# Prologue of a spectral-mixing and MLP kernel: fewer fillers between the parts of x, matrices loaded beside x, two products moved from DVE to Pool, late groups reordered

## The chip, the cores and the metric

One core of one Trainium2 chip. The metric is the device time of one execution in microseconds (us). The profile's span runs from the first to the last instruction; the device time is 1.7 to 2.2 us more.

## The reference, cut to what matters

```python
X = np.fft.rfft(x, axis=1)                 # x: (8, 3008, 256) float32
Y = X * (filt_r + 1j * filt_i)[None]       # filters: (1505, 256)
a = np.fft.irfft(Y, n=3008, axis=1).reshape(24064, 256)
h = a @ w_in                               # 256 -> 2048
out = np.maximum(0.01 * h, h) @ w_out      # 2048 -> 256
```

## The kernel before

The transform of length 3008 = 94 x 32 is done in steps on TensorE: S1 (over 94), a 32x32 transpose T1 on DVE, S2 (over 32, with the f2 matrices), the filter product, SA (back), a transpose T2, SB (back over 94), which writes yt. For batch elements 1 to 7 all that is woven into the steady loop of the two large matmuls. For batch element 0 nothing can hide it: it is the prologue, and the loop's first matmul needs all of its yt. There, the 256 columns are done in two halves (hf 0 and 1), and each half has 24 values of k1 in groups.

```python
first_parts = ((0, 10), (10, 10), (20, 8), (28, 4))
for n0, nn in first_parts:
    x_load(0, n0, nn)                       # Pool queue, float32 to float16
for hf in range(2):
    filt_load(fa_sb, filt_r, hf * DH, DH)   # Pool queue
    filt_load(fb_sb, filt_i, hf * DH, DH)
    for i in (1, 0, 2) if hf == 0 else ():
        nc.gpsimd.dma_start(f2_sb[:, ts(i, NC // FP), :], f2_d.ap()[i])
nc.gpsimd.dma_start(w_in_sb[:], ...)
# ... cut ...
def first_s2(hf, c, n, kind, on_pool=False):    # n matmuls, then products with fa and fb
    ...
    if on_pool:                                 # ACT copies out of PSUM, Pool multiplies
        for j, xf in enumerate(xs):
            act(xf[:], ps[:, ts(j, 4), :])
        for i in range(2):
            for j, xf in enumerate(xs):
                nc.gpsimd.tensor_tensor(y[i][:, ts(j, 4), :], xf[:], fs[i][:, ts(j, 4), :], AL.mult)
    else:
        for i in range(2):
            nc.vector.tensor_tensor(y[i], ps, fs[i], AL.mult)

def first_sa(hf, c, n=4):                       # per 4 k1: two matmuls, one ACT cast
    ...
def upper(hf, t, copy):                         # upper 64 partitions of a filter
    copy(t[64:P, :, ts(hf, DH)], t[0:64, :, ts(hf, DH)])
def keep_warm(n):                               # n matmuls on zeros ("fillers")
    ...

keep_warm(14)
for n0, nn in first_parts:
    ...                                         # S1; copies on DVE and ACT by turns
    keep_warm(5 if n0 < N2 else 14)             # n0 is N2 after the last part
t1_part(0, 0, True)(), t1_part(0, 1, True)()
upper(0, fa_sb, act), upper(0, fb_sb, dve)
first_s2(0, 8, 8, "ph", True)
t1_part(0, 2, True)()
first_s2(0, 0, 8, "ph")
nc.sync.dma_start(i1_sb[:], i1_d.ap())
for n0 in (0, N2 // 2):
    x_load(1, n0, N2 // 2)
t1_part(0, 3, True)()
upper(1, fa_sb, act)
first_s2(0, 16, 4, "pf"), first_s2(0, 20, 4, "pf")
upper(1, fb_sb, dve)
keep_warm(4)
first_s2(1, 0, 8, "ph")
first_sa(0, 0, 8)
first_s2(1, 8, 8, "ph", True)
first_sa(0, 16), first_sa(0, 20), first_sa(0, 8, 8)
first_s2(1, 16, 4, "pf"), first_s2(1, 20, 4, "ph")
first_sa(1, 0, 8)
keep_warm(3)
first_t2(0), first_t2(1)
first_sa(1, 16), first_sa(1, 20), first_sa(1, 8, 8)
first_t2(2), first_t2(3)
# ... SB: 16 groups into yt, casts on ACT and DVE; then the loop ...
```

Of the kernel before, what the change touches and what calls it, by code (L numbers as in the profile page):

```python
# [18 lines left out]
N1, N2 = 94, 32  # L19
NC = 24  # L20
Q = 32
R1 = 96
FP = 3
# [46 lines left out]
def kernel(  # L70
# [9 lines left out]
    nc = tc.nc  # L80
# [12 lines left out]
    f2_d = nc.inline_tensor(f2_np, name="fwd2_const")  # L93
# [4 lines left out]
    f2_sb = cpool.tile([P, NC, P], FP16, name="f2_sb")  # L98
# [22 lines left out]
    def bank(kind, n, w):  # L121
        of = wide if kind == "ph" else single
        t = of[turn[kind] % len(of)]
        turn[kind] += 1
        return t[:, : n * w].rearrange("p (n w) -> p n w", n=n)
# [7 lines left out]
    def x_load(b, n0=0, nn=N2, d0=0, dn=D):  # L133

        for lo, cnt in ((0, R1),) if b + 1 < B else ((0, 64), (64, N1 - 64)):
            nc.gpsimd.dma_start(  # L136
                x_sb[lo : lo + cnt, ds(n0, nn), ds(d0, dn)],
                bass.AP(tensor=x.tensor, offset=x.offset + (b * N + lo * N2 + n0) * D + d0,
                        ap=[[N2 * D, cnt], [D, nn], [1, dn]]))

    def filt_load(dst, src, d0, dn):

        for q, first, sgn in ((0, 0, 1), (Q, N1, -1)):
            nc.gpsimd.dma_start(
                dst[q : q + Q, :, ds(d0, dn)],
                bass.AP(tensor=src.tensor, offset=src.offset + first * D + d0,
                        ap=[[N1 * D, N2 // 2], [sgn * NC * D, 2], [sgn * D, NC], [1, dn]]))


    nc.sync.dma_start(small_sb[:], small_d.ap())  # L150
    first_parts = ((0, 10), (10, 10), (20, 8), (28, 4))
    for n0, nn in first_parts:
        x_load(0, n0, nn)
    for hf in range(2):
        filt_load(fa_sb, filt_r, hf * DH, DH)
        filt_load(fb_sb, filt_i, hf * DH, DH)
        for i in (1, 0, 2) if hf == 0 else ():
            nc.gpsimd.dma_start(f2_sb[:, ts(i, NC // FP), :], f2_d.ap()[i])
    nc.gpsimd.dma_start(w_in_sb[:], moe_w_in.rearrange("(dt p) c -> p dt c", p=P))
    idle = cpool.tile([P, CH], FP16, name="idle")  # L160
    nc.vector.memset(idle[:], 0.0)
# [16 lines left out]
    def paired(t):  # L178
        return t[:].rearrange("p (e n t) -> p n e t", n=Q, t=2)
# [7 lines left out]
    def t1_part(b, i, flat=False):  # L187
        def go():
            a = big[(4 * b) % 3][:].bitcast(FP32)[:, ts(i, E4 * Q)].rearrange("p (e n) -> p e n", n=Q)
            o = big[(4 * b + 1) % 3][:].bitcast(FP32)  # L190
            if flat:
                o = o[:, ts(i, E4 * Q)].rearrange("p (e n) -> p e n", n=Q)
            else:
                o = o.rearrange("p (n e) -> p e n", n=Q)[:, ts(i, E4), :]
            nc.vector.transpose(o, a)  # L195
        return go
# [54 lines left out]
    def first_s1(n0, n, kind, copy):  # L251
        ps = bank(kind, n, D)
        for j in range(0, n, 2):
            nc.tensor.matmul(ps[:, ds(j, 2), :], fwd1[:N1], x_sb[:N1, ds(n0 + j, 2), :],  # L254
                             start=True, stop=True)
        spread(big[0], n0, ps, copy)
# [6 lines left out]
    def first_s2(hf, c, n, kind, on_pool=False):  # L263
        ps = bank(kind, n, DH)
        src = paired(big[1])
        for j in range(n):
            nc.tensor.matmul(ps[:, j, :].rearrange("p (e t) -> p e t", t=2), f2_sb[:, c + j, :],  # L267
                             src[:, c + j, ts(hf, DH // 2)], start=True, stop=True)
        fs = [f[:, ds(c, n), ts(hf, DH)] for f in (fa_sb, fb_sb)]
        y = [prods[hf][:, i, ds(c, n), :] for i in range(2)]  # L270
        if on_pool:
            xs = [scrp.tile([P, 4, DH], FP32, tag=f"p{j // 4 + 1}", name=f"fx_h{hf}_c{c + j}")
                  for j in range(0, n, 4)]
# [9 lines that stand above are left out]
    def first_sa(hf, c, n=4):  # L283
        y = [prods[hf][:, i, ds(c, n), :] for i in range(2)]
        for j in range(0, n, 4):
            ps = bank("pf", 4, DH)
            for i, m in enumerate((inv2, inv2x)):
                nc.tensor.matmul(ps, m, y[i][:, ds(j, 4), :], start=(i == 0), stop=(i == 1))  # L288
            act(paired(big[2])[:, ds(c + j, 4), ts(hf, DH // 2)],
                ps.rearrange("p n (t e) -> p n e t", t=2))  # L290
# [19 lines left out]
    def upper(hf, t, copy):  # L310
        copy(t[64:P, :, ts(hf, DH)], t[0:64, :, ts(hf, DH)])


    def keep_warm(n):
        for _ in range(n):
            nc.tensor.matmul(po_ps.rearrange("p a d -> p (a d)"), idle[:, 0:P], idle[:],  # L316
                             start=True, stop=True)

    keep_warm(14)
    g = 0  # L320
    for n0, nn in first_parts:
        while nn:
            n = 2 if nn % 4 or n0 >= N2 - 4 else 4
            first_s1(n0, n, two[n // 4], (dve, act)[g % 2])
            n0, nn, g = n0 + n, nn - n, g + 1
        keep_warm(5 if n0 < N2 else 14)
    t1_part(0, 0, True)(), t1_part(0, 1, True)()
    upper(0, fa_sb, act), upper(0, fb_sb, dve)
    first_s2(0, 8, 8, "ph", True)
# [2 lines left out]

    nc.vector.memset(i1_sb[:, 0, 0:2], 0.0)
    nc.sync.dma_start(i1_sb[:], i1_d.ap())
    for n0 in (0, N2 // 2):
        x_load(1, n0, N2 // 2)
    t1_part(0, 3, True)()
    upper(1, fa_sb, act)
    first_s2(0, 16, 4, "pf"), first_s2(0, 20, 4, "pf")
    upper(1, fb_sb, dve)  # L340
    keep_warm(4)
    first_s2(1, 0, 8, "ph")
    first_sa(0, 0, 8)
    first_s2(1, 8, 8, "ph", True)
    nc.gpsimd.dma_start(w_out_sb[:], moe_w_out.rearrange("(ct p) d -> p ct d", p=P))
    first_sa(0, 16), first_sa(0, 20), first_sa(0, 8, 8)
    first_s2(1, 16, 4, "pf"), first_s2(1, 20, 4, "ph")
    first_sa(1, 0, 8)
    keep_warm(3)
    first_t2(0), first_t2(1)  # L350
# [118 lines left out]
```

## Time and profile before

| | before |
|---|---|
| median of 3 runs | 780.63 us (780.33 to 781.06) |
| span | 778.8 us |
| first matmul on x | 7.07 |
| T1 starts (the "first transposes") | 14.77 |
| T2 starts (the "last transposes") | 31.57 |
| last copy into yt ends | 39.81 |

The page gives shares over the whole span. Only the engines' timelines, in order of time, tell about a stage of 39 us. A line of a timeline has the start, the duration, the engine, the source line, what it writes from what, how many, and in brackets the idle time before it with what ended it. Line numbers are those of the kernel shown; in the changed kernel the same line stands two or three further down. The profile leaves out the numbers in names: f2_sb stands there as f_sb, i1_sb as i_sb. This one, of TensorE in the kernel before, is worth a look before the prediction: L254 is S1, L316 the fillers.

```profile
7.07 0.38 PE L254 MATMUL pf<-x_sb,small_sb 94*128 94x512 f16 x1 [1.39 <-DMA x_sb<-in_x_dram]
10.38 1.24 PE L316 MATMUL po_ps<-idle 128*128 128x512 f16 x5
11.50 1.02 PE L254 MATMUL ph<-x_sb,small_sb 94*128 94x512 f16 x4
12.36 1.25 PE L316 MATMUL po_ps<-idle 128*128 128x512 f16 x5
13.44 0.60 PE L254 MATMUL pf<-x_sb,small_sb 94*128 94x512 f16 x2
```

The third and fourth parts of x are worked on right behind five fillers, with no wait for a DMA: there the fillers, not x, set the time.

### The profile page before, as it was taken

The numbers are of one execution on the slowest core, as the hardware profiler recorded it, in microseconds if no ns is written. First come the engines' busy times: TensorE is split into PE (matmuls) and PEld (weight loads), VectorE is DVE, ScalarE is ACT, GpSimd is POOL, SyncE is SP. The second block draws the span as 40 slices with busy tenths as digits, with TensorE's granted clock in tenths as the row PEclk, the third lists the DMA queues.
The fourth block names the chain that finished last, engine by engine and source line by source line (L and its number), as shares of the span: only waits on it lengthen the run. The fifth ranks groups of instructions, "written<-read, shape, count | busy, mean of one in ns | idle before, by whom it ended". The sixth has DMA issues, their size and how long they took to land.

```text
span 778.8 us, 13329 instructions
## 1 busy us (share of the span) xinstructions
PE 768.5 (99%) x5688; PEld 521.5 (67%) x5688; DVE 369.6 (47%) x468; ACT 553.5 (71%) x784; POOL 148.7 (19%) x123
## 2 busy tenths in 40 slices
PE   8899999999999999999999999999999999999998
PEld 4556666666776676666777667666667667666666
DVE  5989742765238641576407743187523764200000
ACT  5777768676787768777686775967668676666663
POOL 6854200330005200042002410025000330000000
PEclk9999999999999999999999999999999999999999
DMA  9951013210151010510105010230101010110111
GB/s 186 227 92 56 28 41 71 66 42 29 41 108 42 28 41 28 116 35 28 42 28 122 28 41 29 53 96 28 41 28 42 28 38 31 41 42 28 41 41 55
DMA packets 36154, 43.36 MB, mean 56 GB/s; under 512 B 8130, under 2 KB 34370, under 8 KB 35330
## 3 DMA queue, kind: packets, MB, share of 16 engines
q0 software_dynamic: 10208, 17.01, 12.4%
q1 hardware_dynamic: 25888, 25.52, 9.3%
q8 instruction: 44, 0.72, 0.4%
q14 instruction: 14, 0.11, 0.1%
HBM read 34.10 MB, written 24.64 MB: 75 GB/s over the span
## 4 chain that ended last, share of the span: by engine, by line
PE 96%; DVE 2%; ACT 1%; DMA 1%; issue 0%; DVEq 0%; POOLq 0%
PE ph L377 41%; PE po_ps L391 41%; PE pf L173 3%; PE pf L241 2%; PE pf L213 2%; PE pf L229 2%; PE pf L391 1%; DMA x_sb<-in_x_dram 1%; DVE big L195 1%; DVE prod L281 1%; PE pf L288 0%; ACT big L183 0%; PE po_ps L316 0%; PE ph L267 0%; PE ph L254 0%
## 5 line engine op out<-in xcount | busy, mean ns | idle before, releaser
L382 ACT ACTIVATE gt_c<-ph 128x1024 f16<-128x1024 f32 x376 | 384.9, 1024 | 195.5 <-PE ph L377 193.4
L377 PE MATMUL ph<-yt,w_in_sb 128*128 128x512 f16 (+3 forms) x1600 | 386.6, 367 | 0.3
L391 PE MATMUL po_ps<-w_out_sb,gt_c 128*128 128x256 f16 x2944 | 381.5, 273 | 0.5 <-ACT ost_c_t L398 0.5
L391 PEld LDWEIGHTS <-gt_c 128*128 128x128 f16 x3008 | 290.5, 98 | 82.3 <-issue 2.4
L377 PEld LDWEIGHTS <-w_in_sb 128*128 128x128 f16 x1600 | 154.4, 98 | 97.5 <-issue 0.4
L222 POOL TENSOR_TENSOR y_b_g<-p_b_g,p_b_g 128x512 f16<-128x512 f32 x84 | 106.8, 1272 | 225.7 <-DVE p_b_g L220 225.7
L195 DVE STREAM_TRANSPOSE big<-big 128x1024 f32<-128x1024 f32 x32 | 56.0, 1846 | 126.0 <-ACT big L183 125.9
L183 ACT CAST big<-pf 128x512 f16<-128x512 f32 x186 | 106.6, 605 | 1.1 <-PE pf L254 1.1
L244 DVE CAST yt<-pf 128x376 f16<-128x376 f32 x112 | 56.4, 545 | 86.0 <-PE pf L241 86.0
L218 DVE TENSOR_TENSOR p_b_g<-pf,fa_sb 128x512 f32<-128x512 f32 x84 | 58.1, 692 | 38.3 <-PE pf L213 35.3
L398 ACT COPY ost_c_t<-po_ps 128x256 f32<-128x256 f32 x184 | 69.4, 377 | 6.6 <-PE po_ps L391 5.4
L203 DVE STREAM_TRANSPOSE big<-big 128x1024 f32<-128x1024 f32 x28 | 51.1, 1936 | 34.0 <-ACT big L183 34.0
L219 DVE TENSOR_TENSOR p_b_g<-pf,fb_sb 64x512 f32<-64x512 f32 x84 | 58.2, 692 | 1.1
L220 DVE TENSOR_TENSOR p_b_g<-pf,fb_sb 64x512 f32<-64x512 f32 x84 | 57.4, 683 | 1.1
L136 POOL DMA_DIRECT2D x_sb<-in_x_dram x13 | 7.1, 548 | 253.7 <-PE pf L173 252.9
L241 PEld LDWEIGHTS <-big 128*128 128x128 f16 x448 | 25.7, 98 | 13.2
L173 PE MATMUL pf<-x_sb,small_sb 94*128 94x512 f16 x112 | 33.6, 380 | 0.2 <-DVE yt L244 0.2
L213 PE MATMUL pf<-big,f_sb 128*128 128x256 f16 x168 | 32.1, 273 | 0.0
L229 PE MATMUL pf<-y_b_g,small_sb 128*128 128x512 f16 x84 | 31.9, 380 | 0.0
L213 PEld LDWEIGHTS <-f_sb 128*128 128x128 f16 x168 | 16.4, 98 | 19.7
L241 PE MATMUL pf<-i_sb,big 128*128 128x94 f16 x448 | 28.7, 206 | 0.0
L173 PEld LDWEIGHTS <-small_sb 94*128 94x128 f16 x112 | 10.7, 98 | 10.5
(50 smaller groups left out, 166.8 us busy)
## 6 DMA issues: line engine op xcount, KB each, us to landing
out_dram<-ost_c_t SPq DMA_DIRECT2D x92, 256.0 KB, 2.1
x_sb<-in_x_dram POOLq DMA_DIRECT2D x5, 1536.0 KB, 11.1
x_sb<-in_x_dram POOLq DMA_DIRECT2D x2, 768.0 KB, 12.1
x_sb<-in_x_dram POOLq DMA_DIRECT2D x3, 480.0 KB, 7.3
w_in_sb<-in_moe_w_in_dram POOLq DMA_DIRECT2D x1, 1024.0 KB, 13.3
w_out_sb<-in_moe_w_out_dram POOLq DMA_DIRECT2D x1, 1024.0 KB, 11.8
x_sb<-in_x_dram POOLq DMA_DIRECT2D x1, 1024.0 KB, 8.1
fa_sb<-in_filt_r_dram POOLq DMA_DIRECT2D x4, 192.0 KB, 8.5
```

The costliest lines, as they stand in the source:

```text
L173: nc.tensor.matmul(ps, fwd1[:N1], x_sb[:N1, ds(2 * g, 2), :], start=True, stop=True)
L183: copy(paired(dst)[:, ds(n0, nn), ds(e0, de)], ps.rearrange("p n (e t) -> p n e t", t=2))
L195: nc.vector.transpose(o, a)
L213: nc.tensor.matmul(ps[:, j, :], f2_sb[:, 2 * g + j, :], src[:, 2 * g + j, :], start=True, stop=True)
L218: nc.vector.tensor_tensor(p1[:], ps, fa, AL.mult)
L219: nc.vector.tensor_tensor(p2[0:64], ps[64:P], fb[64:P], AL.mult)
L222: nc.gpsimd.tensor_tensor(y1[:], p1[:], p2[:], AL.add)
L241: nc.tensor.matmul(ps[:, j, :], src[:, dt, n2, :], i1_sb[:, n2, :], start=True, stop=True)
L377: nc.tensor.matmul(ph[:, j, ds(o, ln)], w_in_sb[:, dt, ts(ct, P)], yt[:, dt, ds(lo, ln)], start=(dt == 0), stop=(dt == NDT - 1),)
L382: nc.scalar.activation(gts[ci][:, ds(2 * g, 2), :], ph, AF.Lrelu)
L391: nc.tensor.matmul(po, gts[ci][:, ct, ts(tj, P)], w_out_sb[:, ct, :], start=(ct == 0), stop=(ct == NCT - 1))
L398: nc.scalar.copy(ost[:, tj % 2, :], po)
```

## The change

Its intent: spend fewer fillers where x has landed already; have the S2 matrices early by loading two parts of f2 on the SP queue beside x; relieve DVE of two filter products (k1 = 16 to 19 of the first half) by giving them to Pool; and put the last S2 group, in one wide piece, ahead of the SA groups, so that DVE doesn't wait for it.

```diff
--- before.py
+++ after.py
@@ -148,14 +148,16 @@
 
 
     nc.sync.dma_start(small_sb[:], small_d.ap())
+    for i in (1, 0):
+        nc.sync.dma_start(f2_sb[:, ts(i, NC // FP), :], f2_d.ap()[i])
     first_parts = ((0, 10), (10, 10), (20, 8), (28, 4))
     for n0, nn in first_parts:
         x_load(0, n0, nn)
     for hf in range(2):
         filt_load(fa_sb, filt_r, hf * DH, DH)
         filt_load(fb_sb, filt_i, hf * DH, DH)
-        for i in (1, 0, 2) if hf == 0 else ():
-            nc.gpsimd.dma_start(f2_sb[:, ts(i, NC // FP), :], f2_d.ap()[i])
+        if hf == 0:
+            nc.gpsimd.dma_start(f2_sb[:, ts(2, NC // FP), :], f2_d.ap()[2])
     nc.gpsimd.dma_start(w_in_sb[:], moe_w_in.rearrange("(dt p) c -> p dt c", p=P))
     idle = cpool.tile([P, CH], FP16, name="idle")
     nc.vector.memset(idle[:], 0.0)
@@ -316,14 +318,14 @@
             nc.tensor.matmul(po_ps.rearrange("p a d -> p (a d)"), idle[:, 0:P], idle[:],
                              start=True, stop=True)
 
-    keep_warm(14)
+    keep_warm(18)
     g = 0
-    for n0, nn in first_parts:
+    for (n0, nn), fill in zip(first_parts, (4, 3, 1, 14)):
         while nn:
             n = 2 if nn % 4 or n0 >= N2 - 4 else 4
             first_s1(n0, n, two[n // 4], (dve, act)[g % 2])
             n0, nn, g = n0 + n, nn - n, g + 1
-        keep_warm(5 if n0 < N2 else 14)
+        keep_warm(fill)
     t1_part(0, 0, True)(), t1_part(0, 1, True)()
     upper(0, fa_sb, act), upper(0, fb_sb, dve)
     first_s2(0, 8, 8, "ph", True)
@@ -332,19 +334,20 @@
 
     nc.vector.memset(i1_sb[:, 0, 0:2], 0.0)
     nc.sync.dma_start(i1_sb[:], i1_d.ap())
+    first_s2(0, 16, 4, "pf", True)
     for n0 in (0, N2 // 2):
         x_load(1, n0, N2 // 2)
     t1_part(0, 3, True)()
+    first_s2(0, 20, 4, "pf")
     upper(1, fa_sb, act)
-    first_s2(0, 16, 4, "pf"), first_s2(0, 20, 4, "pf")
     upper(1, fb_sb, dve)
     keep_warm(4)
+    first_s2(1, 8, 8, "ph", True)
     first_s2(1, 0, 8, "ph")
     first_sa(0, 0, 8)
-    first_s2(1, 8, 8, "ph", True)
+    first_s2(1, 16, 8, "ph")
     nc.gpsimd.dma_start(w_out_sb[:], moe_w_out.rearrange("(ct p) d -> p ct d", p=P))
-    first_sa(0, 16), first_sa(0, 20), first_sa(0, 8, 8)
-    first_s2(1, 16, 4, "pf"), first_s2(1, 20, 4, "ph")
+    first_sa(0, 20), first_sa(0, 8, 8), first_sa(0, 16)
     first_sa(1, 0, 8)
     keep_warm(3)
     first_t2(0), first_t2(1)
```

## The prediction

> **What bounds the kernel now.** I read the page first: engine shares, then the chain that ended last, then the costliest groups.
>
> ```profile
> span 778.8 us, 13329 instructions
> PE 768.5 (99%) x5688; PEld 521.5 (67%) x5688; DVE 369.6 (47%) x468; ACT 553.5 (71%) x784; POOL 148.7 (19%) x123
> PE 96%; DVE 2%; ACT 1%; DMA 1%; issue 0%; DVEq 0%; POOLq 0%
> ```
>
> TensorE is busy throughout and carries 96% of the chain. The change touches nothing in the steady loop, only what stands before its first matmul, so the next view is busy time by stretch (columns: stretch, length, busy PE, weight loads, DVE, ACT, Pool with counts, granted clock, DMA share, GB/s).
>
> ```profile
> 17.19:23.73 6.54, 4.53 (x37) 3.73 (x38) 6.51 (x8) 4.14 (x4) 5.87 (x6) 1.00 1.58 198
> 23.73:31.57 7.84, 7.84 (x40) 4.22 (x39) 7.17 (x11) 5.61 (x11) 5.70 (x7) 0.78 1.08 270
> 39.36:778.80 739.44, 734.88 (x5420) 502.47 (x5419) 340.59 (x433) 528.70 (x748) 119.36 (x92) 1.00 0.17 48
> ```
>
> From 39.36 on 739.44 us are TensorE's own, 734.88 of them busy. These don't change; what the change can win or lose is inside the first 39.4 us, and carries to the end one for one. In those stretches DVE is the full one (6.51 of 6.54, 7.17 of 7.84). The chain in order of time says the same for 14.8 to 24 us, then goes over TensorE, DVE and ACT. The timelines of the engines (start, duration, what, idle before and its releaser) fix the points that matter:
>
> ```profile
> 14.07 0.66 ACT L183 CAST big<-pf 128x512 f16<-128x512 f32 x1 [0.48 <-PE pf L254]
> 14.77 2.37 DVE L195 STREAM_TRANSPOSE big<-big 128x1024 f32<-128x1024 f32 x2 [0.21 <-ACT big L183]
> 14.52 0.71 POOL L144 DMA_DIRECT2D fb_sb<-in_filt_i_dram  x1 [0.35 <-DMA fa_sb<-in_filt_r_dram]
> 16.94 1.33 POOL L159 DMA_DIRECT2D w_in_sb<-in_moe_w_in_dram  x1 [0.56 <-DMA fb_sb<-in_filt_i_dram]
> 17.18 2.52 PEld L267 LDWEIGHTS <-f_sb 128*128 128x128 f16 x24 [0.62 <-DMA f_sb<-fwd_const]
> ...
> 29.16 0.69 DVE L281 TENSOR_TENSOR prod<-pf,fa_sb 128x512 f16<-128x512 f32 x1 [0.61 <-PE pf L267]
> 29.97 1.12 ACT L289 CAST big<-pf 128x512 f16<-128x512 f32 x2 [0.65 <-PE pf L288]
> 31.48 2.25 ACT L289 CAST big<-pf 128x512 f16<-128x512 f32 x4 [0.39 <-PE pf L288]
> 31.57 4.61 DVE L296 STREAM_TRANSPOSE big<-big 128x1024 f32<-128x1024 f32 x4
> 34.47 0.85 ACT L308 CAST yt<-pf 128x376 f16<-128x376 f32 x2 [0.73 <-PE pf L305]
> 39.26 0.55 DVE L308 CAST yt<-ph 128x376 f16<-128x376 f32 x1
> ```
>
> The first transposes wait for the last cast of x. Three landings then stand close together: the second half of fa_sb's first columns (Pool is released at 14.52), fb_sb's (16.94, so landed some 0.25 earlier), and the first part of f2 (17.18). DVE copies fb_sb's upper half at 17.17. The last transposes, four in a row, run from 31.57 to 36.18, and the last yt copy ends at 39.81.
>
> **What the Trainium skill says.** "TensorE: Matmul & The Clock Gate", Part 1: the clock is either full or half, judged over free-running windows of about 3.4 us. The trace agrees: 0.50 in all half-microsecond stretches from 24.5 to 27.5, after TensorE idled from 20.86 to 22.87. "DMA: Bandwidth & Descriptors", Queues, rings and completion order: an engine round-robins between the queues that have work, packet by packet. No run here shows it yet for the prologue; it is what the moved f2 loads will meet. "GPSIMD Engine Reference", 4.1 Engine selection: no PSUM access and about 2 times slower than VectorE with two inputs. Here it is 1.13 us against 0.67 for 128x512 (1.7 times), and an ACT copy of 0.53 stands ahead of it.
>
> **The change part by part.** I name the S2 groups by half and first k1, (half, k1).
>
> Zero-tile matmuls. The third part of x has landed when Pool is released at 11.39, the fourth at 12.38; the matmuls on them start at 11.50 and 13.44, behind five fillers of 0.216. With three and one fillers they could start at about 11.2 and 12.5. Then ACT and DVE copies queue (1.23 and 1.03 for wide, 0.66 for narrow), so the first transposes could start at about 13.95 instead of 14.77: 0.82 earlier. Four more fillers at the start end at 6.5, before x.
>
> f2 on the SP queue. Two loads of 256 KB leave before x instead of behind the filters. At the 0.8 us apiece which they take as they arrive in sequence, that is up to 1.3 to 1.6 us of all 16 DMA engines. Between 2 and 4 us only 92 to 101 GB/s move, against some 200 later, so part of it is hidden. I call what remains d and take d = 0.4 (0 to 1.0). All of x and the first filters land d later. The second filters then land about 1.6 - d earlier. That removes f2's wait at 17.18, but fb_sb's landing at 16.7 stays: DVE's upper copy starts at 16.7 + d = 17.1 against 17.17. So the 0.82 of the first step is nearly all lost at that next wait.
>
> k1 = 16 to 19 on Pool. DVE loses two products of 128x512, 1.24 us spacing. Pool gains two of 1.12, ACT one copy of 0.53 at a time when it waited 1.52 for a filter anyway. Pool: start about 18.1 + d, four products 4.45, two 2.24, x loads 1.1, four products 4.5: done at 30.4 + d = 30.8, against 31.16 now.
>
> The wide last group. Four products (29.16 to 31.65, 2.49) become two of 1.23 (2.40). As S2(1,16) now stands ahead of the late SA groups, DVE's 0.61 wait goes. DVE: 17.1, then 5.56 to the end of the fourth transpose (the spacing now, 17.17 to 22.73), 1.18, 0.99, 2.38, 2.40: last transposes could start at 29.6 against 31.57, a gain of 2.0 on DVE alone.
>
> But ACT has still the same twelve casts of SA, 0.58 each, to do after its copies for S2(1,8). The fourth transpose ends at 22.7, eight S2 matmuls take 1.0, ACT's copies 23.9 to 24.9. The first SA cast can start at about 25.4 (0.65 behind its matmul, as at 23.73 to 24.38 now). Then 12 x 0.58 = 7.0, and a hole of 0.7 while TensorE does S2(1,16): ACT ends at 33.1 to 33.3 with a full clock, against 33.73. If the clock is half again after the idle time (20.5 to 22.7 by the same spacing, 2.2 us, as long as now), the four SA matmuls ahead of S2(1,16) cost 1.7 instead of 0.9, and ACT ends at about 34.0. The third of the last transposes needs all of ACT's casts; it starts at 33.3 or 34.0 against 33.87 now.
>
> From there the yt copies: ACT's first eight begin when its SA casts end (33.4 or 34.0 against 34.47), and DVE's begin when the transposes end and a matmul has run, about 0.65 after: 36.25 or 36.95 against 36.92 now. Then 2.89 to the last copy, as now. Sum: 0.65 earlier with the full clock, nothing with the half clock. Even chances of both give 0.3. A mostly later cold window, or d nearer to zero, adds up to 0.5. I put the gain at 0.55, above the plain mean, because the order of SA groups (20, then 8, then 16) looks fitted to when Pool is done and I may have charged ACT's hole too fully. 780.63 - 0.55 = 780.1.
>
> **The rivals.** First, DVE is the bound and its saving arrives whole: 2.0 at the last transposes, 1.5 or so at the loop, 779.0. For it: DVE is the full engine of the prologue and waits just 0.61 in the middle. Against it: ACT's casts end only 0.14 before the third last transpose even now, and their number stays. Second, the f2 loads delay x by the whole 1.3: then everything from the first matmul is 0.9 later than I take, and the time is 780.6 to 781.3. For it: x's packets keep the DMA engines at a share near 1 from 4.5 us on. Against it: the thin stretch at 2 to 4 us. Third, Pool becomes the end of the chain: SA(1,8) waits for its products at 30.4 + d; with d = 1 and the x loads' issue longer, its two casts end at 33.3, so 0.5 of gain remains at most. Fourth, the steady loop shifts, by yt arriving in another order or x's second batch element landing late. Pool issues that at about 25 to 26 instead of 23.4, and it is used from 40.5; the DMA queue is full with w_in until about 30 in any case. I expect nothing of it.
>
> **Range and chances.** The gains of these lie between -0.5 and 1.6, and the three runs of before spread over 0.7 us. So 779.1 to 780.9 should hold it 8 times in 10. Two per cent is 15.6 us, 40% of the whole prologue: nothing here does that. Faster 0.01, same 0.985, slower 0.005.
>
> **What would show it.** The matmuls on x's first part at 7.1 + d; first transposes near 14.3; DVE's upper fb_sb copy waiting for a DMA, near 17.1; no wait of weight loads for f2. DVE's last transposes in two pairs with a gap between, the second pair released by ACT's SA cast, near 33.3 to 34. The loop's first matmuls at about 38.8, against 39.36, and 739.4 us after. I am wrong if the four transposes run without a gap from 30 on (the first rival), if x's first part starts after 7.9 (the second), if the third transpose is released by way of Pool's products, or if the stretch behind the loop's start differs from 739.4 by over 0.3.

## The result, and the profile after

| | before | changed |
|---|---|---|
| median, 4 runs each | 780.48 us (779.75 to 781.06) | 779.99 us (779.97 to 780.97) |
| ratio | | 0.9997, interval 0.998 to 1.0015: same |
| span | 778.8 | 777.8 |
| first matmul on x | 7.07 | 7.60 |
| first transposes | 14.77 | 15.09 |
| last transposes | 31.57, four in a row | 30.29, then 33.67 |
| last copy into yt ends | 39.81 | 39.20 |

A ratio is the mean time of one kernel's fast runs over that of the other's of the same rounds, so it isn't quite the ratio of the medians.

The timeline of TensorE in the changed kernel, at the same places (L256 is S1, L318 the fillers):

```profile
7.60 0.38 PE L256 MATMUL pf<-x_sb,small_sb 94*128 94x512 f16 x1
10.24 0.38 PE L256 MATMUL pf<-x_sb,small_sb 94*128 94x512 f16 x1 [0.53 <-DMA x_sb<-in_x_dram]
12.44 1.02 PE L256 MATMUL ph<-x_sb,small_sb 94*128 94x512 f16 x4 [0.31 <-DVE big L185]
13.52 0.59 PE L256 MATMUL pf<-x_sb,small_sb 94*128 94x512 f16 x2
```

The four parts start 0.53, 0.94, 0.94 and 0.08 later than before. Their landings in the trace say the same: 7.55, 10.19, 12.04 and 12.85, for 7.03, 9.26, 11.11 and 12.10. The fillers have become fewer, and x has become later: the second part is now waited for, and the third waits 0.31 for DVE to empty a bank that the late second part filled.

The timelines of DVE and ACT in the changed kernel, from the first transposes on:

```profile
15.09 2.37 DVE L197 STREAM_TRANSPOSE big<-big 128x1024 f32<-128x1024 f32 x2 [0.20 <-ACT big L185]
17.50 0.95 DVE L313 COPY fb_sb<-fb_sb 64x3072 f16<-64x3072 f16 x1
...
28.01 1.21 DVE L283 TENSOR_TENSOR prod<-ph,fa_sb 128x1024 f16<-128x1024 f32 x1
30.29 2.37 DVE L298 STREAM_TRANSPOSE big<-big 128x1024 f32<-128x1024 f32 x2
33.67 2.37 DVE L298 STREAM_TRANSPOSE big<-big 128x1024 f32<-128x1024 f32 x2 [1.01 <-ACT big L291]
...
28.15 3.14 ACT L291 CAST big<-pf 128x512 f16<-128x512 f32 x6 [0.71 <-PE pf L290]
31.51 2.13 ACT L291 CAST big<-pf 128x512 f16<-128x512 f32 x4 [0.21 <-PE pf L290]
33.62 0.85 ACT L310 CAST yt<-pf 128x376 f16<-128x376 f32 x2
38.65 0.55 DVE L310 CAST yt<-ph 128x376 f16<-128x376 f32 x1
```

DVE's wait for the late S2 group is gone and its last transposes start 1.28 earlier. But they no longer run in a row: the second pair waits 1.01 for ACT's SA casts, and starts about when the third of the four did before. Of 1.28 us won on DVE, 0.61 arrives at the last copy into yt. Two things more are seen in the lines of Pool and of the copies into yt (changed, then before, then changed):

```profile
24.86 1.86 POOL L280 TENSOR_TENSOR prod<-fx_h_c,fb_sb 128x512 f16<-128x512 f32 x1
30.03 2.27 POOL L280 TENSOR_TENSOR prod<-fx_h_c,fb_sb 128x512 f16<-128x512 f32 x2
...
36.92 1.01 DVE L308 CAST yt<-pf 128x376 f16<-128x376 f32 x2 [0.74 <-ACT yt L308]
38.17 0.55 DVE L308 CAST yt<-ph 128x376 f16<-128x376 f32 x1 [0.25 <-PE ph L305]
...
36.66 1.01 DVE L310 CAST yt<-pf 128x376 f16<-128x376 f32 x2 [0.61 <-PE pf L307]
37.58 0.54 DVE L310 CAST yt<-ph 128x376 f16<-128x376 f32 x1
```

Pool's last product ends at 32.30, 1.14 later than before. And of the 0.61, only 0.26 is there when DVE begins its copies into yt. The other 0.35 comes behind that: from there to the end it takes 2.54 in place of 2.89. ACT's first eight copies into yt begin and end 0.85 earlier than before (33.62 to 36.72, for 34.47 to 37.57), so that they are nearly done when DVE's begin, and DVE's wait of 0.25 is gone. All ten profiles with two separate pairs of last transposes have 2.54 or 2.55 here, the four without 2.80 to 2.90.

And the loop? The view of busy time by stretch in the changed kernel:

```profile
23.72:30.29 6.57, 6.57 (x38) 3.84 (x37) 6.51 (x6) 4.42 (x9) 6.56 (x8) 0.78 1.04 259
38.60:777.80 739.20, 734.89 (x5421) 502.41 (x5420) 340.52 (x433) 528.72 (x748) 121.29 (x92) 1.00 0.17 48
```

In the stretch ahead of the last transposes (23.72 to 30.29) Pool is busy for 6.56 of 6.57 us and DVE for 6.51; ACT, the releaser of the second pair, only for 4.42. TensorE's busy time in the loop is the same to 0.01 us. More exactly: from the end of the last copy into yt to the start of the last matmul it is 735.06 us in this profile, in that of before and, within 0.02, in all twelve experiments. So a profile's span is the end of that copy, plus 735.06, plus what follows the last matmul. The latter is 3.89 before and 3.56 in the changed kernel, an item that I come back to. With spans of 778.76 and 777.82 unrounded: 0.61 from the prologue and 0.33 from the program's end. Yet the device times of the two profiled runs, 780.54 and 779.99, differ by 0.55 only: what lies outside the span is 1.78 in the one and 2.17 in the other.

### The profile page after: what moved, and what is told of

Read it like the earlier page. It is cut to its first block, busy times and chain, and to the rows that moved or that the text cites. A ratio compares the mean times of both kernels' runs of the same rounds, so it can differ in the third digit from the quotient of the medians.

```text
span 777.8 us, 13325 instructions
## 1 busy us (share of the span) xinstructions
PE 768.4 (99%) x5685; PEld 521.3 (67%) x5685; DVE 368.4 (47%) x464; ACT 553.7 (71%) x785; POOL 149.9 (19%) x123
## 3 DMA queue, kind: packets, MB, share of 16 engines
HBM read 34.10 MB, written 24.64 MB: 76 GB/s over the span
## 4 chain that ended last, share of the span: by engine, by line
PE 95%; DVE 1%; ACT 1%; DMA 1%; issue 0%; POOL 0%; DVEq 0%; POOLq 0%
PE ph L380 41%; PE po_ps L394 41%; PE pf L175 3%; PE pf L243 2%; PE pf L215 2%; PE pf L231 2%; DMA x_sb<-in_x_dram 1%; PE pf L394 1%; PE pf L290 1%; PE ph L269 1%; ACT big L185 1%; DVE big L197 0%; DVE big L298 0%; DVE prod L283 0%; ACT big L291 0%
```

## The experiments

All were correct. Each was run five times beside the kernel before on the same chip; there were three batches, each on a chip of its own, and before with the half-clock window has means of 780.76, 780.68 and 780.77 on them. The landmarks of their profiles, in us (T0 is the start of the first transposes, "end" that of the last copy into yt, "rest" the time after the last matmul's start up to the span's end):

| profile | clock window | first matmul on x | T0 | last transposes | end | T0 to end | rest |
|---|---|---|---|---|---|---|---|
| before | half | 7.07 | 14.77 | 31.57, no gap | 39.81 | 25.04 | 3.89 |
| before_warm | full | 7.37 | 15.08 | 31.24, no gap | 39.49 | 24.41 | 3.90 |
| f2_alone | full | 7.74 | 15.68 | 31.83, no gap | 40.07 | 24.39 | 3.78 |
| changed | half | 7.60 | 15.09 | 30.29, 33.67 | 39.20 | 24.11 | 3.56 |
| again | half | 7.97 | 15.08 | 30.49, 33.90 | 39.42 | 24.34 | 3.56 |
| warm | full | 8.05 | 15.36 | 30.55, 33.68 | 39.22 | 23.86 | 3.56 |
| f2_old | full | 6.84 | 13.96 | 29.71, 32.84 | 38.37 | 24.41 | 3.68 |
| fill_old | half | 7.71 | 15.67 | 30.90, 34.31 | 39.85 | 24.18 | 3.56 |
| pool_old | half, twice as long | 7.67 | 14.99 | 32.02, 35.42 | 40.95 | 25.96 | 3.56 |
| pool_late | half | 7.79 | 15.15 | 31.74, 34.45 | 39.98 | 24.83 | 3.56 |
| order_old | half | 7.73 | 15.08 | 32.11, no gap | 40.35 | 25.27 | 3.55 |
| sa_dve | half | 7.95 | 15.22 | 30.71, 34.10 | 39.63 | 24.41 | 3.56 |
| best | full | 7.08 | 14.20 | 30.08, 32.79 | 38.33 | 24.13 | 3.68 |
| best_tail | full | 6.88 | 13.99 | 29.88, 32.59 | 38.12 | 24.13 | 3.33 |

"Half" means that the trace records 3.41 us of half clock in the prologue (6.83 in pool_old). Medians, and the ratio to the kernel before in the same rounds: again 780.21 (0.9998), f2_old 779.35 (0.9987), fill_old 780.59 (1.0001), pool_old 781.15 (1.0009), warm 779.85 (0.9992), before_warm 779.98 (0.9993), pool_late 780.47 (1.0003), best 779.01 (0.9981), f2_alone 780.83 (1.0009), order_old 780.67 (1.0003), sa_dve 780.02 (0.9996), best_tail 778.52 (0.9977). The intervals of f2_old, best and best_tail alone lie wholly below 1 (up to 0.9999, 0.9993, 0.9989). Smaller effects rest on the profiles' landmarks and on the groups of runs. Sorted by clock, the means are, with the half-clock window: before 780.73, changed 780.28, f2_old 779.55, fill_old 780.65, pool_late 780.71, order_old 780.87, sa_dve 780.12; at full clock: before 779.85, f2_old 779.29, best 779.00. Some of these groups have only two to four runs.

### again: the changed kernel, unedited

> The changed kernel once more, unedited, for the spread. The four runs so far are 779.97, 779.98, 779.99 and 780.97, those of the kernel before 779.75 to 781.06. If the phase of the clock's windows against the start of the kernel is what parts them (one theory), the times fall in two or three groups about 0.5 to 1 us apart in both kernels, and a profile in another group has its half-clock window elsewhere. If it is noise of the chip (the rival), they scatter evenly. Median expected at 780.0, ratio to before 0.9993, interval within 0.998 to 1.001.

Measured 780.11 to 780.77, all with a clock of 0.997 or 0.998. The kernel before gave two groups in this batch: 779.48, 779.55 and 779.70 at a clock of 1.000, and six from 780.53 to 781.06 at 0.997 to 0.998. Over all 27 runs of before with a known clock: ten at full clock with a mean of 779.85 and 17 with the half-clock window with a mean of 780.73. All nine of the changed kernel have the window; their mean is 780.28. So against before in the same clock, the changed kernel is 0.45 faster; against the mixture, 780.41, only 0.13. In the second profile of the changed kernel the window stands 0.90 later (24.13 against 23.23), and DVE's copy of fb_sb waits for its load, as predicted, which it had not done in the first:

```profile
15.08 2.37 DVE L197 STREAM_TRANSPOSE big<-big 128x1024 f32<-128x1024 f32 x2 [0.23 <-ACT big L185]
17.68 0.95 DVE L313 COPY fb_sb<-fb_sb 64x3072 f16<-64x3072 f16 x1 [0.23 <-DMA fb_sb<-in_filt_i_dram]
```

### f2_old: the f2 loads back on the Pool queue

```diff
-    for i in (1, 0):
-        nc.sync.dma_start(f2_sb[:, ts(i, NC // FP), :], f2_d.ap()[i])
-        if hf == 0:
-            nc.gpsimd.dma_start(f2_sb[:, ts(2, NC // FP), :], f2_d.ap()[2])
+        for i in (1, 0, 2) if hf == 0 else ():
+            nc.gpsimd.dma_start(f2_sb[:, ts(i, NC // FP), :], f2_d.ap()[i])
```

> The changed kernel, with the f2 loads put back behind the filters on the Pool queue; new fillers, Pool group and order stay. My theory: the f2 loads on the SP queue cost x its landings 0.5 to 0.95 us, so here the first transposes start at about 13.95 (15.09 in the changed kernel), weight loads of S2 wait for f2 until about 17.1, and DVE's upper copy starts at about 16.95 (17.50). Last yt copy ends about 0.4 to 0.5 earlier than the 39.20 of the changed kernel, so about 38.75 and 779.5. Rival: x's delay is the launch-to-launch state of the memory and not f2, then the first transposes stay at 15.1 or so and S2 starts when they end.

```profile
13.96 2.37 DVE L195 STREAM_TRANSPOSE big<-big 128x1024 f32<-128x1024 f32 x2 [0.22 <-ACT big L183]
16.53 0.95 DVE L311 COPY fb_sb<-fb_sb 64x3072 f16<-64x3072 f16 x1 [0.20 <-DMA fb_sb<-in_filt_i_dram]
16.96 1.92 PE L267 MATMUL ph<-big,f_sb 128*128 128x128 f16 x16 [0.97 <-DMA f_sb<-fwd_const]
32.84 2.37 DVE L296 STREAM_TRANSPOSE big<-big 128x1024 f32<-128x1024 f32 x2 [0.77 <-ACT big L289]
```

The lines of DVE and TensorE in this run confirm the direction, and the transposes to the tenth: they start at 13.96, and the wait for f2, 0.97 here, is back. The copy of fb_sb (16.53) and the end (38.37) come 0.4 earlier than I expected. Undoing this part makes the changed kernel 0.86 faster (median 779.35 against 780.21 of the same batch). Part of that could be the clock, which was full in the profile; but the three runs with a half-clock window have a mean of 779.55 against 780.32 of again, where all have it: still 0.77. The fillers' gain does exist, then: it shows when f2 isn't in x's way. It isn't the whole 0.82, though. The transposes start 0.81 earlier than in before, of which 0.23 is x itself, landing earlier in this profile; from the first matmul on x to the transposes it takes 7.70 in before and 7.12 here, in best and in best_tail 7.11. So the fillers give 0.58.

How the loads meet can be counted in the trace's records of DMA packets of the changed kernel (not a view of the profile, so a plain table; queue, packets, KB and median time of one, in the half microsecond from the time given; some left out):

```
from     x and filters (Pool queue)      constants (SP queue)
2.5      none                            46 packets,  92 KB,  84 ns
3.0      13 packets,  65 KB, 560 ns      69 packets, 112 KB,  84 ns
4.0      18 packets,  90 KB, 398 ns      16 packets,  32 KB,  96 ns
5.0      16 packets,  80 KB, 449 ns      14 packets,  28 KB,  96 ns
6.0      17 packets,  55 KB, 398 ns      22 packets,  44 KB,  96 ns
7.0      21 packets,  90 KB, 398 ns      19 packets,  24 KB,  84 ns
```

Once x's packets of 5120 bytes are there, f2's of 2048 bytes go beside them in about equal numbers, until nearly 8 us: about 16 of each in half a microsecond, which is what 16 engines give that take turns one by one (0.398 + 0.096 is 0.49 us for a pair). The trace doesn't tell the engine of a packet, so the turns are inferred from these counts. The first f2 load is issued at 1.14, ahead of x, and lands at 4.25. The second is issued at 1.61, behind x's first part (1.24), and lands at 8.63, also behind it (7.55): it takes 0.1 us of every half one, spread over all of x's first part and some of its second.

### fill_old: the old fillers

```diff
-    keep_warm(18)
+    keep_warm(14)
-    for (n0, nn), fill in zip(first_parts, (4, 3, 1, 14)):
+    for (n0, nn), fill in zip(first_parts, (5, 5, 5, 14)):
```

> The changed kernel with the old fillers (14, then 5 5 5). My theory: with x's parts landing as late as they do in the changed kernel, fillers 5 after the first and second part end as x lands and cost about 0 to 0.1, the third 5 delays the last two matmuls on x by four fillers, 0.86. First transposes at about 15.9 to 16.0 (15.09), last yt copy 0.7 to 0.9 later than 39.20, time 780.8. Rival: the DMA landings of the filters gate what follows anyway, then the end moves by under 0.3.

T0 is 15.67, 0.58 later than in the changed kernel and not 0.8 to 0.9, and the end 0.65 or 0.43 later than in the changed kernel's two profiles; the median is 0.38 above again's. The bound had shifted: in the changed kernel DVE's copies had already eaten part of what fewer fillers give. The rival, under 0.3, falls.

### pool_old and pool_late: k1 = 16 to 19 on DVE again

```diff
# pool_old
-    first_s2(0, 16, 4, "pf", True)
+    first_s2(0, 16, 4, "pf")
# pool_late
-    first_s2(0, 16, 4, "pf", True)
     ...
     t1_part(0, 3, True)()
-    first_s2(0, 20, 4, "pf")
+    first_s2(0, 16, 4, "pf"), first_s2(0, 20, 4, "pf")
```

> The changed kernel with k1 = 16 to 19 on DVE again, as before. Rival that DVE is the bound: its 1.24 us come back whole, the last yt copy ends at about 40.4 and the time is 781.2. My theory that ACT's twelve SA casts bind: ACT loses a copy of 0.53 that stood in a wait, Pool ends 2.2 earlier, DVE's last transposes run without a gap from about 31.5 to 36.1, which is where the second pair ends now (36.04): the last yt copy moves by 0 to 0.3, time 780.0 to 780.3. Third theory, that Pool binds the last SA groups (its products end at 32.25 in the changed kernel, and the last casts at 33.64): then the last casts come up to 1 us earlier.

This was a miss: the end came 1.75 later than in the changed kernel, more than the 1.24 of the products themselves. I had put the products ahead of the fourth transpose, where the changed kernel's code has the group; in the kernel before they stood behind it. Everything of the second half hangs on that transpose: it started at 23.18 in place of 21.90. And with the longer idle time of TensorE the half-clock window was twice as long. The run answers another question than I meant to ask. So the next puts them where they had been:

> The run pool_old put the products of k1 = 16 to 19 on DVE ahead of the fourth transpose, which the kernel before did not: its last yt copy ended at 40.95, 1.75 later than in the changed kernel, and all S2 of the second half came 1.28 later. Here they are on DVE behind that transpose, as before. If the fourth transpose and what follows (S2, ACT copies, casts) is the bound, and DVE's sum is not, the last yt copy ends within 0.4 of 39.2 and the median is 780.0 to 780.4. If DVE's sum is the bound, 1.2 later: 781.2, as pool_old.

End 39.98, 0.78 or 0.56 later than the two profiles of the changed kernel; median 780.47 against 780.21. It lies between: not the 1.24 of DVE's sum, and not within 0.4. The last transposes start 1.25 later than in again, the second pair 0.55 later:

```profile
31.74 2.36 DVE L298 STREAM_TRANSPOSE big<-big 128x1024 f32<-128x1024 f32 x2
34.45 2.37 DVE L298 STREAM_TRANSPOSE big<-big 128x1024 f32<-128x1024 f32 x2 [0.35 <-ACT big L291]
32.29 2.13 ACT L291 CAST big<-pf 128x512 f16<-128x512 f32 x4 [0.57 <-PE pf L290]
```

These lines of DVE and ACT in pool_late show how: ACT now waits 0.57 ahead of its last four casts, for products that DVE ends later. About half of what DVE saves passes through; the other half had been the wait for ACT.

### warm and before_warm: is it the clock?

```diff
-    keep_warm(4)
+    keep_warm(12)
```

> The changed kernel with twelve zero-tile matmuls instead of four in the idle time of TensorE ahead of the second half's S2 groups (21.2 to 23.2 in its trace). Theory: nine runs of the kernel before fell into two groups, 779.48 to 779.70 at a mean granted clock of 1.000 and 780.53 to 781.06 at 0.997 to 0.998, while all nine of the changed kernel had 0.997 to 0.998; so the half-clock window in the prologue costs about 0.6 to 1.1, and the changed kernel always has it. Then here the clock stays full in most runs, the first pair of SA casts comes 0.15 behind the matmuls, the last yt copy 0.6 earlier than 39.2, median 779.4. Rival: casts and products bind, the clock alone gives under 0.2: median 779.9 to 780.1 at clock 1.000.

> The kernel before with the same twelve instead of four. If the half-clock window is what parts its two groups, all runs fall in the faster one: median 779.5, clock 0.999 to 1.000, spread under 0.3. If the groups come from something else (landings of the loads), two groups stay, with full clock in both.

In all ten runs the clock is 0.999 to 1.000. The window goes away, so the idle time of TensorE ahead of the second half's S2 is its cause. Its worth differs: before goes from 780.73 (window) to 779.97 on average, changed from 780.28 to 779.90. For before I had expected a spread under 0.3; it is 0.7 (779.60 to 780.31), so the clock isn't the only thing that varies. Where x's first part lands varies too: matmuls on it start at 6.84 to 7.37 in the five kernels without early f2, and at 7.60 to 8.05 in the nine with it. For warm the result, 0.3 to 0.4, lies between theory (0.6) and rival (under 0.2). The TensorE and Pool lines of warm tell what stopped it:

```profile
30.31 2.28 POOL L280 TENSOR_TENSOR prod<-fx_h_c,fb_sb 128x512 f16<-128x512 f32 x2
32.64 0.38 PE L290 MATMUL pf<-prod,small_sb 128*128 128x512 f16 x1 [0.49 <-POOL prod L280]
33.05 0.60 ACT L291 CAST big<-pf 128x512 f16<-128x512 f32 x1 [0.33 <-PE pf L290]
33.68 2.37 DVE L298 STREAM_TRANSPOSE big<-big 128x1024 f32<-128x1024 f32 x2 [0.78 <-ACT big L291]
```

With the full clock ACT is no longer the bound: the last SA matmul waits 0.49 for Pool's last product, ACT 0.33 for that matmul, and DVE for ACT. Comparing equal clocks, warm at 779.90 and before_warm at 779.97 are the same within their spread: at full clock the whole change is worth nothing measurable in device time. (The mean spans differ by 0.38, about what the program's end gives; the time outside the span takes most of it back.)

### order_old: the old order of the second half's groups

```diff
-    first_s2(1, 8, 8, "ph", True)
     first_s2(1, 0, 8, "ph")
     first_sa(0, 0, 8)
-    first_s2(1, 16, 8, "ph")
-    first_sa(0, 20), first_sa(0, 8, 8), first_sa(0, 16)
+    first_s2(1, 8, 8, "ph", True)
+    first_sa(0, 16), first_sa(0, 20), first_sa(0, 8, 8)
+    first_s2(1, 16, 4, "pf"), first_s2(1, 20, 4, "ph")
     first_sa(1, 0, 8)
```

> The changed kernel with the old order of the second half's S2 and SA groups and with the last S2 group in two narrow pieces; fillers, f2 and Pool's group stay. Theory: DVE waits again for the late S2 group (0.61 before) and does four narrow products in 2.49 for 2.27, so the last transposes start at 31.0 to 31.3 (30.29), and as the first SA casts stand ahead of ACT's copies for (1, 8), the last SA cast ends 0.1 to 0.5 later than 33.64; last yt copy 0.3 to 0.6 later than 39.2, median 780.4. Rival: ACT has twelve casts in either order and comes to the same end: median 780.0 to 780.1.

```profile
29.71 0.69 DVE L283 TENSOR_TENSOR prod<-pf,fa_sb 128x512 f16<-128x512 f32 x1 [1.64 <-PE pf L269]
32.11 4.61 DVE L298 STREAM_TRANSPOSE big<-big 128x1024 f32<-128x1024 f32 x4
```

The direction is right and the size short: DVE's wait is 1.64 and not 0.6 (its product starts at 29.71 behind it), the last transposes start at 32.11, and the end is 40.35, 0.9 to 1.15 later. The median is 0.46 above again's, with two of its five runs at full clock (780.22 and 780.27; the three others 780.67 to 781.04). With Pool's new group in place the old order is a little worse than it was in the kernel before (25.27 from T0 to the end, against 25.04). Of the parts that were undone, this is the one that pays most: 0.59 with the half-clock window in both, against 0.43 for Pool's group (pool_late, with one run of 781.82 in it) and 0.37 for the fillers, by the means above.

### f2_alone: the f2 loads on the SP queue, in the kernel before

```diff
+    for i in (1, 0):
+        nc.sync.dma_start(f2_sb[:, ts(i, NC // FP), :], f2_d.ap()[i])
-        for i in (1, 0, 2) if hf == 0 else ():
-            nc.gpsimd.dma_start(f2_sb[:, ts(i, NC // FP), :], f2_d.ap()[i])
+        if hf == 0:
+            nc.gpsimd.dma_start(f2_sb[:, ts(2, NC // FP), :], f2_d.ap()[2])
```

> The kernel before with one part of the change alone: two f2 loads on the SP queue ahead of x, fillers and order as before. Theory: these loads cost x 0.7 at its first part and about as much at the last (first matmuls on x at 7.6 to 8.05 in six traces with them, 6.84 to 7.37 in four without), so the first transposes start at 15.6 to 15.8 (14.77 and 15.08 before) and the last yt copy ends 0.4 to 0.9 later than 39.81: a median of 781.0 to 781.4 if the half-clock window comes, less 0.35 that the program's end gains, for the stores' semaphores fall on other numbers (3.56 from the last matmul to the end, against 3.89). Rival: f2's late landing at 17.1 was as much of a bound as x, so its removal pays for x's delay: median as before, 780.5.

T0 is 15.68, as expected. Three runs at full clock, 780.70 to 780.83, against 779.85 for before at full clock; two with the window, 781.41 and 781.50, against 780.73. In either clock this part alone costs 0.7 to 0.9. The rival, that f2's early landing pays for x's delay, falls: behind T0 nothing is won (24.39 to the end, against 24.41 in before_warm at the same clock). The rest after the last matmul was 3.78, so 0.11 less than before and not the 0.33 that I had counted in.

### sa_dve: one of ACT's SA casts on DVE

```diff
-    first_sa(1, 16), first_sa(1, 20), first_sa(1, 8, 8)
+    first_sa(1, 16), first_sa(1, 20), first_sa(1, 8, 8, dve)   # its last cast on DVE
```

> The changed kernel with the last of ACT's twelve SA casts on DVE, between the two pairs of last transposes, where DVE waits 1.01. If ACT's casts bind there, ACT is free at 33.1 and not 33.64, DVE's cast ends at 33.35, the second pair starts at 33.4 (33.67) and the yt copies 0.3 to 0.5 earlier: median 779.7. If Pool's products (ending at 32.3) or DVE bind, nothing changes or DVE's cast of 0.69 comes on top: 780.0 to 780.5.

Median 780.02, and one run at full clock with 779.52; the end is 39.63. No gain:

```profile
33.30 0.69 DVE L291 CAST big<-pf 128x512 f16<-128x512 f32 x1 [0.22 <-PE pf L290]
34.10 2.37 DVE L298 STREAM_TRANSPOSE big<-big 128x1024 f32<-128x1024 f32 x2
```

DVE, free earlier, waits for the last SA matmul, and its cast is longer than ACT's. Pool's last product ends at 32.41 in this trace and that matmul runs from 32.60. So even at half clock Pool and ACT stand within a few tenths of one another, and taking work off ACT alone brings nothing measurable.

### best and best_tail: what the traces point to

The core of the edit to the changed kernel (best), and the one line of best_tail:

```diff
# loads, all on the Pool queue: x, fa (half 0), f2 parts 1 and 0, fb (half 0), f2 part 2, fa, fb (half 1)
-    keep_warm(18)
+    keep_warm(14)
# order:
+    for i in range(4):
+        t1_part(0, i, True)()
     upper(0, fa_sb, act), upper(0, fb_sb, dve)
     first_s2(0, 8, 8, "ph", True)
     first_s2(0, 0, 8, "ph")
+    late = first_s2(1, 8, 8, "ph", True)   # matmuls and ACT copies now, Pool's products later
     first_s2(0, 16, 4, "pf", True)         # its copy in a buffer of its own
     first_s2(0, 20, 4, "pf")
     upper(1, fa_sb, act), upper(1, fb_sb, dve)
+    late()
+    for n0 in (0, N2 // 2):
+        x_load(1, n0, N2 // 2)             # behind Pool's products
+    keep_warm(6)
     first_s2(1, 0, 8, "ph")
     first_sa(0, 0, 8)
     first_s2(1, 16, 8, "ph")
# best_tail
-    nc.sync.dma_start(i1_sb[:], i1_d.ap())
+    for lo, hi in [(0, 5), (5, 9), (9, 14), (14, 18), (18, 23), (23, 27), (27, 32)]:
+        nc.sync.dma_start(i1_sb[:, lo:hi, :], i1_d.ap()[:, lo:hi, :])
```

> A version from what the traces show. Loads on the Pool queue in the order x, fa_sb's first half, two parts of f2, fb_sb's first half, third part of f2; the four transposes first on DVE; ACT's copies for (1, 8) early, Pool's products ahead of x's next loads. Theory: the bound is the chain landing, transposes, S2, ACT's copies and casts, Pool's products; the x landings are those of the kernel before (first transposes at 13.95), the third of the last transposes starts at about 32.0 (33.67 in the changed kernel, 32.84 in f2_old), the last yt copy ends at about 37.7 and the median is 778.6. Rival that DVE's sum binds: DVE has as much to do as in f2_old, from 13.95 on with 0.3 less of gaps, so 38.0 and 779.0. Rival that the DMA landings bind: fb_sb's first half lands 1.6 later and Pool's third product waits for it, then the end is that of f2_old, 779.35.

Median 779.01, full clock in all five runs, 1.2 below the changed kernel and 1.6 below before's median of that batch (780.62). Part of this is the clock: at full clock in both, it is 0.9 below warm (779.90) and below before (three runs of that batch, 779.92). The third of the last transposes started at 32.79 and not at 32.0: DVE's four late products end at about 30.1 and the last four SA casts come only after them, so the rival that DVE's sum binds named the median (779.0) better than I did.

> The kernel of the run best with the load of i1 in seven pieces, so that the last store uses the eighth of the SP queue's semaphores and not the second. At the end SyncE waits for the eight one after the other, some 0.062 each, from the last landing on. Theory: six waits fewer behind the last landing, so from the last matmul to the end 3.3 to 3.35 instead of 3.68, and the median 0.3 below best's 779.01: 778.7. Rival: the end is set by other engines' drains; then 3.6 to 3.7 stays. The start of the second pair of last transposes should stay at 32.8.

```profile
32.59 2.37 DVE L301 STREAM_TRANSPOSE big<-big 128x1024 f32<-128x1024 f32 x2 [0.35 <-ACT big L294]
37.57 0.55 DVE L313 CAST yt<-ph 128x376 f16<-128x376 f32 x1
```

The rest after the last matmul is 3.33, within the expected range. SyncE's waits at the program's end, from the trace's records, in us after the start of the last matmul (the last store lands at 2.40 or 2.41 in all):

```
before     1.08 1.15 | 2.42 2.48 2.54 2.60 2.66 2.72 2.78
changed    1.08 1.15 1.22 1.28 | 2.42 2.48 2.54 2.60 2.66
best_tail  1.09 1.17 1.24 1.31 1.38 1.75 1.82 1.89 | 2.43
```

Each wait on another of the queue's semaphores takes some 0.06. They are done in one fixed order, so those that stand behind the last store's own wait for nothing and still cost. Two more loads on the SP queue, the f2 of the change, moved that store's semaphore by two places: 0.12. The other 0.21 of the difference between before (3.89) and changed (3.56) is a drain of DVE among the last instructions: in before it takes 0.120 in place of 0.019 and ends late, at 3.68, after Pool's at 3.45. best has the same waits as before without the late drain, and 3.68. Why it is late isn't shown. The median of best_tail, 778.52, is the lowest of all; the prologue ended 0.21 earlier too in its profile, so the program's end is shown by the landmarks, not by the median.

## Why the prediction was right, point by point

The number: 780.1 predicted, 779.99 measured as the median of four, 780.28 as the mean of the nine runs.

- **The bound.** Right: the loop stayed as it was, and the prologue's end carries over one for one (735.06 in all fourteen profiles).
- **d, the delay of x by f2.** Mis-sized: taken as 0.4; x's four parts landed 0.52, 0.93, 0.93 and 0.75 later. The step that failed is the sum of up to 1.3 to 1.6 us of DMA time less what the thin stretch hides. Only the first f2 load left before x. The second didn't fill a hole and then leave; it took turns with x through the whole first part. So the first transposes came at 15.09, not 14.3, and later than before. By the prediction's own sign for its second rival, a first part after 7.9, the first profile says no (7.60) and again says yes (7.97). That the fillers' gain would be lost was right; the reason given, fb_sb's landing, holds in again (a wait of 0.23) and not in the first profile, where the transposes themselves were the later. The gain itself was 0.58, not 0.82.
- **DVE's saving.** 2.0 predicted at the last transposes, 1.28 measured; the difference is the later start (15.09 + 2.37 = 17.46, for 17.1) and DVE's copy of fb_sb's second half, which took 1.37 for 0.95 while Pool was at work.
- **ACT's casts in the way.** Right that they hold up the second pair of transposes: 33.67, with a wait of 1.01 for ACT. The times were less exact than they look: 34.0 was forecast for the end of the casts with the half clock, and they ended at 33.64; 33.1 to 33.3 with the full clock, and in warm they ended at 33.65.
- **Pool.** Its sum failed: done at 30.8 was forecast, and its last product ends at 32.30. It started at 19.26 in place of 18.5, as the transposes came late, and the product that met DVE's copy of fb_sb took 1.86 in place of 1.12. So ACT isn't alone: warm, f2_old and sa_dve show Pool's last product right ahead of the last SA matmul. My third rival is thus half true, and at full clock Pool is the one waited for.
- **The copies into yt.** "Then 2.89 to the last copy, as now" failed: it was 2.54. This is more than half of the 0.61 that the prologue gained in the profiled pair, and the prediction had nothing of it.
- **The clock.** Right that the window matters; the size depends on the pair. From before with the window (780.73) to warm at full clock (779.90) it is 0.83, where I had said 0.65; within the changed kernel (780.28 to 779.90) it is 0.38. The even chances were wrong: the changed kernel had the window in nine of nine runs, before in 17 of 27. With the window in both, 0.45 was measured where I had forecast no gain. In the span it is 0.78 (means of 778.89 and 778.11); 0.33 of that comes from the program's end, which I hadn't looked at, and the time outside the span takes as much back.
- **Rivals.** That DVE's saving arrives whole is out (779.0). That x is late by the whole 1.3 is out too, but in its second and third parts x was nearer to it than to my 0.4.
- **What cancels.** Within the profiled pair: 0.61 from the prologue, 0.33 from the end, 0.39 given back outside the span, 0.55 in sum. That the sum is the 0.55 that I predicted is luck: for what happened, the half clock in both, my sum was no gain at all, and the 0.55 came from averaging with the full clock and adding a quarter of a microsecond.

What stays open: why the time outside the span is about 1.8 in some kernels and 2.15 in others (before's runs have 1.74 to 1.94, the changed one's 2.11 to 2.21; those of best and best_tail spread from 1.91 to 2.14); no part of the change explains it: sa_dve differs from the changed kernel in the place of one cast and has 1.74 to 1.84. Nor do I know why the window is so certain in the changed kernel; its idle time on TensorE, 21.18 to 23.20, is as long as before's.

## What to carry to other kernels

A load put on another queue ahead of the critical one isn't out of its way: here they took turns packet by packet, and the critical load was later by up to 0.93 us, more than half of the 1.3 to 1.6 that I had estimated for the other. In a short stage that several engines share, taking work off the fullest one uncovers the next after some tenths: find, for the last wait, which two or three producers end within that distance, before moving work. When times fall in groups, sort the runs by granted clock before comparing kernels; the change here gains 0.45 us or nothing depending on which group one compares with.

## What the Trainium skill lacked or had wrong

- "DMA: Bandwidth & Descriptors", Queues, rings and completion order: the counts agree with its turns by packet (from 4 to 7 us 14 to 24 packets of x's queue and 14 to 22 of f2's in each half microsecond), but the page doesn't say what an early small load costs the other one: here 0.7 to 0.9 us for 512 KB (f2_alone).
- "TensorE: Matmul & The Clock Gate", Part 1: the half clock is said to come after an idle window of about 3.4 us. Here some 2 us of idle time were enough. In before, the window from 20.92 to 24.33, whose later 1.46 of 3.41 us had matmuls (43%), was followed by the half clock; one of 3.85 to 7.26, with 2.0 busy (59%), was not. Cut into windows the same way, the prologues of the fourteen traces have 33 to 44% in the eight windows that ended the full clock, and 54% or more in all those at full clock that kept it. (In pool_old one of 59%, begun at half clock, was followed by half clock again.) The page doesn't say which share is enough. That the windows' phase differs from run to run agrees with the page (first full clock recorded at 3.85, 4.47, 6.16 and 7.06).
- None of the pages consulted has the cost of the waits at a program's end on the SP queue's semaphores, one after the other at 0.06 us each, so that the number of loads and stores on that queue matters: six waits fewer behind the last landing took it from 3.68 (best) to 3.33 (best_tail) from the last matmul's start to the span's end.
